# Every load and store on SyncE's queue, and a table in place of the list scheduler

## The chip, the cores and the metric

The kernel runs on one core of a Trainium2 chip. The metric is device time in microseconds of one execution; the median of several runs is compared. PE is TensorE, DVE VectorE, ACT ScalarE, POOL GpSimd, SP SyncE.

## The reference

Three stages follow one another on two batches of 768 positions and 512 channels.

```python
# 1: attention with 8 heads of 64; a score counts only where the 6 hash bits agree
q_bucket = sum((q @ proj > 0) * 2**arange(6));  k_bucket likewise
s = where(q_bucket == k_bucket, q @ k.T / 8, -1e9)
x = softmax(s) @ v
# 2: four causal attentions (experts) of 64 channels, weighted by a top-2 gate
for e in range(4):
    a = softmax(causal((x @ wq[e]) @ (x @ wk[e]).T / 8))
    out += gate_e * (a @ (x @ wv[e]) @ wo[e])
# 3: mix with the position before, square of relu, and a sigmoid gate
xk = mu_k * x + (1 - mu_k) * x_prev;   xr = mu_r * x + (1 - mu_r) * x_prev
return sigmoid(xr @ w_r) * (maximum(xk @ w_k, 0)**2 @ w_v)
```

The weights w_k, w_r and w_v of the third stage come in double precision, all else in single.

## The kernel before

The work is cut into twelve units of 128 positions (six for each batch). For each unit there are four lists of steps: the query (`query_steps`: load, hash, turn), the hashed attention (`lsh_steps`, eight heads), the experts (`moe_steps`, four heads) and the mixing (`mix_steps`: hidden layer h, gate r, down projection v). Matmul operands are split into a high and a low half of 16 bits, and each product is three matmuls. Keys and values of a batch are prepared by `key_steps`, the weights by `split_w` (single precision) and `split_d` (double precision; loads of 512 KB into the tile `raw`, of which there are two).

A head goes through `softmax`: PE writes its scores to PSUM (tile s, or se for an expert), DVE evicts them with the row's extreme (P), ACT takes the exponential (P again, with the row's sum), ACT (in two heads of eight POOL) makes the high half and POOL the low half (PHL), and a DMA transpose on SP's queue makes PT, the stationary operand of the product with v (tile x, or y for an expert). There are four buffers of P, six of PHL, three of PT. Names like PT_5_0 mean unit 5, head 0; PT_m3_1 is unit 3, expert 1; the last number in an order's row is a running number.

Nothing is issued while the steps are run: `Program.add` records each instruction as an `Op` with what it depends on (matmuls of one step in a row form one Op; 2673 in all). Before, `Program.plan` then runs a list scheduler: it has a cost for each Op (`cost`), a due time for each step (`times`, with numbers in `CONF`) and a model of the queues, and leaves a sequence in `self.order`. `issue` emits the Ops in that sequence, each to its engine's queue, where they run in order; all instructions therefore carry the line of `issue` (L396) in the profile, and are told apart by their tiles.

Three switches in CONF name the queue of the DMAs: all 2, which is ACT's.

```python
QS = [nc.sync, nc.gpsimd, nc.scalar]
def DQ():      # weights
    return QS[CONF["dq"]]
def LQ(i):     # keys, values and queries: SP for what comes first
    return QS[CONF["lq"]] if i else nc.sync
def OQ():      # outputs
    return QS[CONF["oq"]]
```

Of the kernel before, what the change touches and what calls it, by code (L numbers as in the profile page):

```python
# [131 lines left out]
class Op:  # L132

    __slots__ = ("eng", "calls", "prio", "uses", "after", "before", "step", "ahead", "left", "ready", "end", "dur", "dma", "lock",
                 "table", "tiles")


class Program:
# [3 lines left out]
    def __init__(self, nc):  # L142
        self.nc, self.ops, self.ahead, self.last, self.share = nc, [], (), None, 1.0
        self.step = Step(self, None)
        self.step.at = -3.0
# [4 lines left out]
    def add(self, engine, method, args, kw):  # L150
# [4 lines left out]
        if not (eng == "PE" and o is not None and o.eng == "PE" and o.step is self.step):  # L155
            o = Op()
            o.eng, o.calls, o.uses, o.step, o.ahead = eng, [], {}, self.step, self.ahead
            o.after, o.dur, o.dma, o.lock, o.table = set(), 0.0, 0.0, False, None
            self.ops.append(o)
            self.last = o  # L160
        o.calls.append((engine, method, args, kw))
        self.cost(o, method, args, kw, views)
# [17 lines left out]
    def switch(self, ns):  # L180

        self.last.dur += ns

    def cost(self, o, method, args, kw, views):

        n = max((v.ids.size for v, _ in views), default=1)
        psum = any(v.tile.pool.psum for v, _ in views)
        ins = [v for v, w in views if not w and v.ids.size > 1]
        if o.eng == "PE":
            x = args[2] if method == "matmul" else args[1]  # L190
            cols = x.ids.size if method == "matmul" else 128
            o.dur += max(cols / 2.4 * (2 if x.dt == F32 else 1) + 2.5, 26.0) * self.share * 1.015
        elif method.startswith("dma_start"):
            v = views[0][0]
            size = v.ids.size * mybir.dt.size(v.dt)
            if method == "dma_start":
                dram = next(a for a in args if not isinstance(a, View))
                run = dram.ap[-1][1] * mybir.dt.size(dram.dtype)
                o.dur, o.dma = 60.0, 250.0 + size * 128 * 2.67e-3 * (1.5 if run <= 256 else 1.0) + (600.0 if run <= 16 else 0.0)
            else:  # L200
                o.dur, o.dma = 1100.0 + size / 256 * 27.0, size / 256 * 150.0
        elif o.eng == "DVE":
            rate = 1.043
            if not psum and len(ins) < 2 and "accum_out" not in kw and method in ("tensor_scalar", "tensor_copy"):
                rate = 0.53 if any(v.dt == F32 for v in ins) else 0.26
                o.lock = n > 1
            elif method == "tensor_copy" and all(v.dt == F16 for v, _ in views):
                rate = 0.53
            elif not psum and len(ins) > 1:
                o.lock = True  # L210
            o.dur = (143.0 if n > 20 else 140.0) + rate * n + (80.0 if "accum_out" in kw else 0.0) - 78.0
        elif o.eng == "ACT":
            o.dur = (150.0 if psum else 190.0) + 0.83 * n + (187.0 if "accum_out" in kw else 0.0) - 94.0
            f = args[2] if method == "activation" else None
            o.table = f if f in (AF.Exp, AF.Sigmoid) else None
        elif o.eng == "POOL":
            o.dur = 147.0 + (1.9 if len(ins) > 1 else 0.85) * n
            o.lock = True

    def plan(self, conf):  # L220

        window, wait = conf["win"], conf["wait"]
        lat = {"DVE": 130.0, "ACT": 145.0, "POOL": 135.0, "PE": 75.0, "SP": 60.0}
        for o in self.ops:
            o.before, o.left, o.ready = [], len(o.after), 0.0
            o.prio = o.step.at - sum(conf[a] for a in o.ahead)
            o.tiles = [t for t in o.uses if t.slot]
            for t in o.tiles:
                t.users = 0
        free, queue, opened = {}, {}, set()  # L230
        for o in reversed(self.ops):
            for q in o.after:
                q.before.append(o)
                q.prio = min(q.prio, o.prio - 1e-6)
        for o in self.ops:
            for t in o.tiles:
                t.users += 1
                if t not in opened:
                    opened.add(t)
                    free.setdefault(t.slot, [0.0] * t.bufs)  # L240
                    queue.setdefault(t.slot, []).append((o.prio, len(opened), t))
        for q in queue.values():
            q.sort(key=lambda a: a[:2], reverse=True)
        ends = {t: 0.0 for t in opened}
        held = set()
        todo = {e: [] for e in lat}
        clock = {e: 0.0 for e in lat}
        lock = 0.0
        slow, frame, busy = False, 0, {}
        table = AF.Exp  # L250
        order = []

        now, lines, coming, lanes = 0.0, ([], []), [], []
        inf = float("inf")

        def done(o, end):
            o.end = end
            for q in o.before:
                q.left -= 1
                q.ready = max(q.ready, end + (-170.0 if q.eng == o.eng == "PE" else lat[q.eng]))  # L260
                if not q.left:
                    l = todo[q.eng]
                    k = len(l)
                    while k and l[k - 1].prio > q.prio:
                        k -= 1
                    l.insert(k, q)
            for t in o.tiles:
                t.users -= 1
                ends[t] = max(ends[t], end)
                if not t.users:  # L270
                    free[t.slot].append(ends[t])

        for o in self.ops:
            if not o.left:
                todo[o.eng].append(o)
        for l in todo.values():
            l.sort(key=lambda o: o.prio)
        while len(order) < len(self.ops):
            best = None
            for e, l in todo.items():  # L280
                pick = None
                for o in l[:window]:
                    at = max(clock[e], o.ready)
                    if pick is not None and at + wait.get(e, 0.0) >= pick[0]:
                        continue
                    if o.dma:
                        if len(lanes) >= 7:
                            if not lanes[-7].end:
                                continue
                            at = max(at, lanes[-7].end)  # L290
                        if e == "SP" and sum(1 for d in lanes[-6:] if not d.end and d.eng == "SP") > 2:
                            continue
                    new = [t for t in o.tiles if t not in held]
                    if len(new) == 1:
                        t = new[0]
                        if not free[t.slot] or queue[t.slot][-1][2] is not t:
                            continue
                        at = max(at, min(free[t.slot]))
                    for t in new if len(new) > 1 else ():
                        same = [u for u in new if u.slot == t.slot]  # L300
                        if len(free[t.slot]) < len(same) or any(a[2] not in same for a in queue[t.slot][-len(same):]):
                            at = None
                            break
                        at = max(at, sorted(free[t.slot])[len(same) - 1])
                    if at is None:
                        continue
                    if pick is None or at + wait.get(e, 0.0) < pick[0]:
                        pick = (at, o)
                if pick and (best is None or pick[0] < best[0]):
                    best = pick  # L310

            limit, landed = best[0] if best else inf, None
            while landed is None and (lines[0] or lines[1] or coming):
                rate = 0.42 if lines[0] and lines[1] else 1.0
                step, kind = limit - now, None
                for k in (0, 1):
                    if lines[k] and lines[k][0][0] / rate <= step:
                        step, kind = lines[k][0][0] / rate, k
                if coming and max(coming[0][0] - now, 0.0) <= step:
                    step, kind = max(coming[0][0] - now, 0.0), 2  # L320
                if kind is None:
                    for k in (0, 1):
                        if lines[k]:
                            lines[k][0][0] -= max(step, 0.0) * rate
# [854 lines left out]
```

## Time and profile before

| | |
|---|---|
| median of 3 runs | 524.77 us (524.51 to 527.95) |
| span of the profiled execution | 523.5 us; its own time was not noted apart, the median is 1.3 us more |
| PE busy | 443.3 us, 85% |
| DVE busy | 378.4 us, 72% |
| ACT busy | 349.1 us, 67% |
| POOL busy | 311.6 us, 60% |

A busy share is a mean over the whole span. The kernel has a start in which keys, values and weights are brought in and split, a long middle in which all twelve units overlap, and a short end; which engine sets the time differs between them, so the shares have to be read by stages. The idle time of an engine that nobody waits for costs nothing.

### The profile page before, as it was taken

The page shows a single profiled execution, that of the slowest core. Times are in us where ns is not written, and L with a number is a line of the kernel's source. Part 1 is how long each engine was busy: PE and PEld are TensorE (multiplying, and loading weights), DVE is VectorE, ACT ScalarE, POOL GpSimd, SP SyncE. Part 2 cuts the span into 40 slices and gives each one's busy share as a digit, 9 for nine tenths or more (in the row PEclk, how much of TensorE's full clock was granted, in tenths as well). Part 3 has the DMA queues.
Part 4 walks back from the last instruction along what each step waited for, and adds up shares of the span by engine and source line. Part 5 has one row for each costly group of instructions (what it writes and reads, how often), then busy time and mean ns, then how long its engine had stood idle before and what let it go on. Part 6 is the DMA issues. An engine that isn't in the chain of part 4 may idle for free.

```text
span 523.5 us, 15721 instructions
## 1 busy us (share of the span) xinstructions
PE 443.3 (85%) x6288; PEld 335.6 (64%) x6288; DVE 378.4 (72%) x1094; ACT 349.1 (67%) x660; POOL 311.6 (60%) x286
## 2 busy tenths in 40 slices
PE   1666655486679899898898999998999999998997
PEld 1644454374466685685777678786786867876764
DVE  2789878688889958766987976866857687376432
ACT  3358855677777857956378977886665978558231
POOL 5879762755756934946464693962936568374110
PEclk9977879878899999999899999999999999999999
DMA  8749979599879996998479889496554889847200
GB/s 245 185 123 172 241 168 221 131 196 193 134 140 207 152 172 87 150 191 147 107 162 155 163 140 163 96 183 99 118 111 90 132 149 174 126 84 117 68 23 20
DMA packets 225243, 75.08 MB, mean 143 GB/s; under 512 B 216593, under 2 KB 220817, under 8 KB 225169
## 3 DMA queue, kind: packets, MB, share of 16 engines
q1 hardware_dynamic: 198288, 52.19, 60.0%
q10 hardware_dynamic: 26880, 21.88, 15.9%
q8 instruction: 49, 0.80, 0.6%
q14 instruction: 26, 0.20, 0.1%
HBM read 22.14 MB, written 3.15 MB: 48 GB/s over the span
## 4 chain that ended last, share of the span: by engine, by line
PE 40%; DMA 15%; DVE 13%; issue 9%; ACT 9%; POOL 7%; SPq 1%; ACTq 0%; POOLq 0%; DVEq 0%
DMA PT<-PHL 9%; PE h L396 8%; PE v L396 7%; PE s L396 5%; DMA PT_m<-PHL_m 5%; PE x L396 4%; PE r L396 4%; POOL PHL L396 3%; PE qk L396 3%; POOL PHL_m L396 2%; DVE P L396 2%; ACT P L396 2%; PE tr_x L396 2%; PE o L396 1%; DVE P_m L396 1%
## 5 line engine op out<-in xcount | busy, mean ns | idle before, releaser
L396 POOL TENSOR_TENSOR PHL<-P,PHL 128x768 f16<-128x768 f32 x96 | 159.1, 1667 | 56.2 <-ACT PHL L396 48.9
L396 DVE TENSOR_SCALAR_CACHE_REDUCE P<-s 128x768 f32<-128x768 f32 x96 | 91.1, 952 | 22.7 <-PE s L396 16.7
L396 ACT ACTIVATE P<-P,mx 128x768 f32<-128x768 f32 x96 | 89.1, 929 | 27.4 <-DVE mx L396 26.4
L396 PE MATMUL s<-y,x 128*128 128x384 f16 x384 | 81.7, 342 | 18.0 <-DVE P L396 13.4
L396 PE MATMUL x<-v,PT 128*128 128x64 f16 x1728 | 68.9, 197 | 11.4 <-DMA PT<-PHL 9.2
L396 PEld LDWEIGHTS <-PT 128*128 128x128 f16 x1728 | 63.6, 101 | 21.9 <-DMA PT<-PHL 12.7
L396 PE MATMUL h<-mk,WK 128*128 128x128 f16 x1152 | 74.7, 219 | 2.5 <-POOL mk L396 1.9
L396 PE MATMUL v<-WV,k 128*128 128x512 f16 x288 | 71.7, 379 | 0.7 <-DVE kT L396 0.7
L396 PEld LDWEIGHTS <-WK 128*128 128x128 f16 x1152 | 67.7, 98 | 7.0 <-issue 2.3
L396 PEld LDWEIGHTS <-x 128*128 128x128 f16 x576 | 42.0, 100 | 46.0 <-issue 24.9
L396 POOL TENSOR_TENSOR PHL_m<-P_m,PHL_m 128x128 f16<-128x128 f32 (+5 forms) x48 | 48.9, 1037 | 29.2 <-ACT PHL_m L396 28.6
L396 ACT ACTIVATE PHL<-P 128x768 f16<-128x768 f32 x72 | 59.8, 835 | 6.8 <-DMA PT_m<-PHL_m 4.1
L396 PE MATMUL qk<-xT,WQK 128*128 128x128 f16 x576 | 42.8, 229 | 3.6 <-DVE xT L396 1.9
L396 PEld LDWEIGHTS <-WQK 128*128 128x128 f16 x576 | 37.5, 103 | 6.8 <-issue 4.6
L396 PEld LDWEIGHTS <-k 128*128 128x128 f16 x288 | 26.1, 98 | 23.1 <-DVE kT L396 0.8
L396 ACT ACTIVATE P_m<-P_m,bias_m 128x128 f32<-128x128 f32 (+5 forms) x48 | 31.7, 660 | 11.2 <-DVE P_m L396 11.2
L396 PE MATMUL r<-WR,mr 128*128 128x512 f16 x144 | 36.6, 379 | 0.7 <-DVE e L396 0.7
L396 DVE TENSOR_SCALAR_CACHE_REDUCE P_m<-se 128x128 f32<-128x128 f32 (+5 forms) x48 | 28.6, 617 | 6.7 <-PE se L396 5.0
L396 ACT ACT_TABLE_LOAD x20 | 25.7, 1283 | 10.1 <-DMA consts<-in_consts_dram 7.1
L396 POOL TENSOR_TENSOR mr<-m32r,mr 128x512 f16<-128x512 f32 x12 | 13.9, 1159 | 30.4 <-ACT mr L396 30.4
L396 PE MATMUL y<-vn,PT_m 128*128 128x64 f16 x504 | 22.6, 195 | 8.5 <-DMA PT_m<-PHL_m 8.5
L396 PEld LDWEIGHTS <-PT_m 128*128 128x128 f16 x504 | 19.9, 99 | 14.7 <-DMA PT_m<-PHL_m 10.4
(127 smaller groups left out, 808.3 us busy)
## 6 DMA issues: line engine op xcount, KB each, us to landing
raw_k<-in_moe_w_k_dram ACTq DMA_DIRECT2D x8, 512.0 KB, 4.9
raw_v<-in_moe_w_v_dram ACTq DMA_DIRECT2D x8, 512.0 KB, 5.2
out_dram<-e ACTq DMA_DIRECT2D x12, 256.0 KB, 2.3
q<-in_q_dram ACTq DMA_DIRECT2D x11, 256.0 KB, 5.2
raw_r<-in_moe_w_r_dram ACTq DMA_DIRECT2D x4, 512.0 KB, 3.9
k<-in_k_dram SPq DMA_DIRECT2D x4, 384.0 KB, 6.0
v<-in_v_dram SPq DMA_DIRECT2D x4, 384.0 KB, 4.0
PT<-PHL SPq DMA_TRANSPOSE x96, 4.7
```

The costliest lines, as they stand in the source:

```text
L396: getattr(getattr(self.nc, engine), method)(*[real(a) for a in args], **{k: real(a) for k, a in kw.items()})
```

## The change

Two things change. All loads of weights, keys, values and queries, and the twelve stores of the output, are issued on SP's queue, on which the transposes are too: 66 DMAs leave ACT's queue, which keeps six small ones (the hash's projection, constants, mu). And the list scheduler goes, with its costs, due times and CONF; a table of 2673 numbers gives the sequence of the Ops. The Ops, their tiles and what they depend on are the same in both, and so are the numbers of instructions of each engine, except that ACT's table loads are 18 and no longer 20.

```diff
+    def arrange(self, table):
+        places = np.frombuffer(zlib.decompress(base64.b85decode("".join(table.split()))), np.uint16)
+        self.order = [self.ops[i] for i in places]
...
-    def LQ(i):
-        return QS[CONF["lq"]] if i else nc.sync
...
+    LOADS = nc.sync
...
         for dap, sap in src_dmas:
-            DQ().dma_start(dap(w32), sap)
+            LOADS.dma_start(dap(w32), sap)
...
-        DQ().dma_start(raw.rearrange("p n a -> p (n a)"), src.bitcast(U32))
+        LOADS.dma_start(raw.rearrange("p n a -> p (n a)"), src.bitcast(U32))
...
-                OQ().dma_start(out[b, s0:s0 + P, :], o)
+                LOADS.dma_start(out[b, s0:s0 + P, :], o)
...
-    nc.plan(CONF)
+    nc.arrange(ORDER)
...
+ORDER = """
+c-jrsgMwf=5CFhN(n-IyZQJ(D+O}=mwr$(CZQHi(y{n%nfiOT&0MY_L2FL>p=^#B6hrD3GLVhR=86gwo1BA@rAPW?Mq7VY1;30s5PzXwaLTQ)?lb{4lh
...
```

On SP's queue, this stood in a row where unit 1's heads are transposed, before:

```order
L396 DMA_TRANSPOSE PT_1_0_878<-PHL_1_0_788 128x12x128
L396 DMA_TRANSPOSE PT_1_1_908<-PHL_1_1_828 128x12x128
L396 DMA_TRANSPOSE PT_1_2_939<-PHL_1_2_842 128x12x128
L396 DMA_TRANSPOSE PT_1_3_1055<-PHL_1_3_882 128x12x128
L396 DMA_TRANSPOSE PT_1_4_1097<-PHL_1_4_886 128x12x128
L396 DMA_TRANSPOSE PT_1_5_1149<-PHL_1_5_942 128x12x128
L396 DMA_TRANSPOSE PT_1_6_1217<-PHL_1_6_973 128x12x128
L396 DMA_TRANSPOSE PT_1_7_1300<-PHL_1_7_997 128x12x128
L396 DMA_TRANSPOSE PT_m0_0_1360<-PHL_m0_0_1236 128x2x128
L396 DMA_TRANSPOSE PT_m0_1_1395<-PHL_m0_1_1243 128x2x128
```

and now, from the sixth of that unit's heads on:

```order
L188 DMA_TRANSPOSE PT_1_5_1095<-PHL_1_5_960 128x12x128
L188 DMA_TRANSPOSE PT_1_7_1180<-PHL_1_7_954 128x12x128
L188 DMA raw_r0_0_1199<-in_moe2_w_r_dram 128x1024
L188 DMA_TRANSPOSE PT_1_0_1242<-PHL_1_0_893 128x12x128
L188 DMA_TRANSPOSE PT_1_4_1297<-PHL_1_4_1097 128x12x128
L188 DMA raw_r1_0_1300<-in_moe2_w_r_dram 128x1024
L188 DMA_TRANSPOSE PT_1_3_1336<-PHL_1_3_1059 128x12x128
L188 DMA_TRANSPOSE PT_1_2_1376<-PHL_1_2_1111 128x12x128
L188 DMA raw_r2_0_1409<-in_moe2_w_r_dram 128x1024
L188 DMA_TRANSPOSE PT_m0_1_1449<-PHL_m0_1_1280 128x2x128
L188 DMA_TRANSPOSE PT_m0_0_1459<-PHL_m0_0_1360 128x2x128
L188 DMA raw_r3_0_1479<-in_moe2_w_r_dram 128x1024
```

Loads of the gate's weights (raw_r, 512 KB each) now stand between the transposes, and the heads of a unit come in another sequence. Over the whole queue 29 loads stand ahead of the first transpose (nine before; five of the 29 are of raw_k), and behind it fifteen weight loads of 512 KB, loads of queries, keys and values and the twelve stores stand between transposes.

On PE's queue, this stood before between the scores of unit 5's head 0 (s_5_0) and the first matmul that reads a PT of that unit (one row of each step; weight loads and repeated rows are left out):

```order
L396 MATMUL s_5_0_3341<-y1_0_0_418,x1_5_3048 128x384
...
L396 MATMUL vg_3_3348<-WVG_234,xT_3_2913 128x260
...
L396 MATMUL s_5_1_3364<-y1_0_0_418,x1_5_3048 128x384
...
L396 MATMUL v_1_3260<-WV2_1925,k2_1_2929 128x512
...
L396 MATMUL se_3_1_3390<-kT_0_1125,qT_3_3142 128x512
...
L396 MATMUL s_5_2_3404<-y1_0_0_418,x1_5_3048 128x384
...
L396 MATMUL h_2_0_3437<-mk_2_3308,WK2_655 128x128
...
L396 MATMUL s_5_3_3455<-y1_0_0_418,x1_5_3048 128x384
...
L396 MATMUL s_5_4_3477<-y1_0_1_254,x1_5_3048 128x384
...
L396 MATMUL y_3_3484<-vn_0_1181,PT_m3_0_3410 128x64
...
L396 MATMUL s_5_5_3544<-y1_0_1_254,x1_5_3048 128x384
...
L396 MATMUL x_5_3594<-v_0_0_399,PT_5_0_3464 128x64
```

and now, for the head that this unit uses first, head 7:

```order
L188 MATMUL s_5_7_3340<-y1_0_1_300,x1_5_2746 128x384
...
L188 MATMUL x_4_3015<-v_0_0_269,PT_4_3_3315 128x64
...
L188 MATMUL h_1_4_3405<-mk_1_2566,WK2_208 128x128
...
L188 MATMUL s_5_2_3439<-y1_0_0_400,x1_5_2746 128x384
...
L188 MATMUL s_5_5_3521<-y1_0_1_300,x1_5_2746 128x384
...
L188 MATMUL vg_4_3544<-WVG_442,xT_4_3512 128x260
...
L188 MATMUL s_5_6_3569<-y1_0_1_300,x1_5_2746 128x384
...
L188 MATMUL v_1_3332<-WV2_1806,k2_1_3131 128x512
...
L188 MATMUL qk_4_3599<-xT_4_3512,WQK_272 128x128
...
L188 MATMUL s_5_3_3689<-y1_0_0_400,x1_5_2746 128x384
...
L188 MATMUL o_3_3707<-yT_3_3687,WO_195 128x128
...
L188 MATMUL x_5_3782<-v_0_1_387,PT_5_7_3765 128x64
```

More steps of other units, mixing (h, v), projections (qk, vg, o) and products of unit 4's heads (x_4), lie between a head's scores and its product.

On DVE's queue, the first evictions of unit 0 stood before so:

```order
L396 TENSOR_SCALAR P_0_0_491,mx_0_492<-s_0_0_479 128x768
L396 TENSOR_SCALAR P_0_1_500,mx_0_492<-s_0_1_485 128x768
L396 TENSOR_SCALAR mx_0_492<-mx_0_492 128x1
L396 SCALAR_TENSOR_TENSOR naq_1_503<-q32_1_396,naq_1_503 128x8x64
L396 TENSOR_SCALAR mx_0_492<-mx_0_492 128x1
L396 TENSOR_SCALAR P_0_2_519,mx_0_492<-s_0_2_495 128x768
L396 SCALAR_TENSOR_TENSOR v_0_1_305<-v32_0_1_1_416,v_0_1_305 128x768
L396 TENSOR_SCALAR mx_0_492<-mx_0_492 128x1
L396 TENSOR_SCALAR P_0_3_547,mx_0_492<-s_0_3_510 128x768
```

and now so:

```order
L188 TENSOR_SCALAR P_0_2_437,mx_0_438<-s_0_2_423 128x768
L188 TENSOR_SCALAR P_0_0_444,mx_0_438<-s_0_0_432 128x768
L188 TENSOR_SCALAR mx_0_438<-mx_0_438 128x1
L188 TENSOR_SCALAR wd_k20_0_461<-wm_k20_0_398 128x512
L188 TENSOR_SCALAR mx_0_438<-mx_0_438 128x1
L188 COPY x1_0_366<-tr_x1_0_312 128x512
L188 COPY x2_1_466<-tr_x2_1_446 128x512
L188 TENSOR_SCALAR P_0_3_473,mx_0_438<-s_0_3_468 128x768
L188 COPY x2_1_466<-tr_x2_1_446 128x512
L188 COPY y1_0_0_400<-tr_y1_0_0_0_1_478 128x768
L188 SCALAR_TENSOR_TENSOR wd_k20_0_461<-raw_k20_0_372,wd_k20_0_461 128x512
```

Work on the weights of the hidden layer (wd_k) has moved in among the first evictions, and the splitting of values and of the next query out of them.

## Rows read from the trace of the kernel before

**Rows 1.** The page's first part: busy time, share and instructions of each engine.
```profile
PE 443.3 (85%) x6288; PEld 335.6 (64%) x6288; DVE 378.4 (72%) x1094; ACT 349.1 (67%) x660; POOL 311.6 (60%) x286
```

**Rows 2.** Busy time by stages; columns: stage, its length, engines, granted clock, DMA, GB/s.
```profile
0.00:32.00 32.00, 14.20 (x226) 12.86 (x227) 17.56 (x40) 11.55 (x16) 22.27 (x31) 0.94 0.77 200
32.00:157.00 125.00, 82.99 (x1094) 62.19 (x1092) 104.92 (x280) 87.68 (x174) 81.97 (x77) 0.85 0.86 174
157.00:497.00 340.00, 323.34 (x4756) 245.73 (x4753) 247.69 (x759) 243.24 (x460) 205.05 (x177) 0.99 0.79 136
497.00:524.00 27.00, 22.80 (x221) 14.80 (x219) 8.22 (x17) 6.62 (x11) 2.32 (x2) 0.98 0.06 21
```

**Rows 3.** Waits of PE, 0 to 160 us: total, times, longest.
```profile
PE s L396 <- DVE P L396: 12.8, 13, 2.0
...
PE y L396 <- DMA PT_m<-PHL_m: 4.6, 2, 2.4
PE x L396 <- DMA PT<-PHL: 4.3, 3, 2.1
```

**Rows 4.** Waits of PE, 157 to 524 us, the longest three.
```profile
PE x L396 <- DMA PT<-PHL: 4.9, 6, 1.2
PE y L396 <- DMA PT_m<-PHL_m: 4.0, 5, 1.5
PE tr_y L396 <- DVE nbk L396: 1.4, 1, 1.4
```

**Rows 5.** The chain, 30 to 160 us: its shares and two pieces (start, length).
```profile
by line: issue 18.3%; POOL PHL L396 11.0%; DMA PT_m<-PHL_m 8.2%; DMA raw_v<-in_moe_w_v_dram 5.5%; DVE P L396 4.7%; ACT P L396 4.7%; DVE wd_k L396 4.3%; DMA PT<-PHL 4.1%; DVE wd_r L396 2.8%; ACT PHL L396 2.5%; PE s L396 2.0%; DVE x L396 1.9%
...
88.62 4.51 issue
...
142.76 7.09 DMA raw_v<-in_moe_w_v_dram
```

**Rows 6.** The page's groups: busy, mean ns, idle before with what ended it.
```profile
L396 POOL TENSOR_TENSOR PHL<-P,PHL 128x768 f16<-128x768 f32 x96 | 159.1, 1667 | 56.2 <-ACT PHL L396 48.9
L396 DVE TENSOR_SCALAR_CACHE_REDUCE P<-s 128x768 f32<-128x768 f32 x96 | 91.1, 952 | 22.7 <-PE s L396 16.7
L396 ACT ACTIVATE P<-P,mx 128x768 f32<-128x768 f32 x96 | 89.1, 929 | 27.4 <-DVE mx L396 26.4
L396 PE MATMUL s<-y,x 128*128 128x384 f16 x384 | 81.7, 342 | 18.0 <-DVE P L396 13.4
L396 PE MATMUL x<-v,PT 128*128 128x64 f16 x1728 | 68.9, 197 | 11.4 <-DMA PT<-PHL 9.2
...
L396 PE MATMUL h<-mk,WK 128*128 128x128 f16 x1152 | 74.7, 219 | 2.5 <-POOL mk L396 1.9
L396 PE MATMUL v<-WV,k 128*128 128x512 f16 x288 | 71.7, 379 | 0.7 <-DVE kT L396 0.7
...
L396 ACT ACTIVATE PHL<-P 128x768 f16<-128x768 f32 x72 | 59.8, 835 | 6.8 <-DMA PT_m<-PHL_m 4.1
```

**Rows 7.** The tile PT: its transposes on SP (min/median/max ns), and issue to landing.
```profile
L396 SPq DMA_TRANSPOSE PT<-PHL x96: 1413/1600/6159, 40.0 to 451.9; - x96
...
DMA to landing us min/median/max: 3.6/4.7/9.4
```

**Rows 8.** The tile raw_v: its loads on ACT's queue, same columns.
```profile
L396 ACTq DMA_DIRECT2D raw_v<-in_moe_w_v_dram x8: 334/335/363, 113.2 to 163.1; - x8
```

**Rows 9.** The page's groups: loads of ACT's function table.
```profile
L396 ACT ACT_TABLE_LOAD x20 | 25.7, 1283 | 10.1 <-DMA consts<-in_consts_dram 7.1
```

**Rows 10.** Waits of SP's queue, 30 to 160 us, the longest.
```profile
SPq L396 <- PE x L396: 40.6, 14, 9.7
```

More of the change, by code (lines that the diff above doesn't have):

```diff
@@ L1 @@
+import base64
+import zlib
 from contextlib import ExitStack
@@ L132 @@
 class Op:
-    __slots__ = ("eng", "calls", "prio", "uses", "after", "before", "step", "ahead", "left", "ready", "end", "dur", "dma", "lock",
-                 "table", "tiles")
+    __slots__ = ("eng", "calls", "uses", "after", "step")
 class Program:
@@ L142, in __init__ @@
     def __init__(self, nc):
-        self.nc, self.ops, self.ahead, self.last, self.share = nc, [], (), None, 1.0
+        self.nc, self.ops, self.last = nc, [], None
         self.step = Step(self, None)
-        self.step.at = -3.0
     def __getattr__(self, name):
@@ L156, in add @@
             o = Op()
-            o.eng, o.calls, o.uses, o.step, o.ahead = eng, [], {}, self.step, self.ahead
-            o.after, o.dur, o.dma, o.lock, o.table = set(), 0.0, 0.0, False, None
+            o.eng, o.calls, o.uses, o.step = eng, [], {}, self.step
+            o.after = set()
             self.ops.append(o)
@@ L178, in add @@
                 log.append((o, m))
[L180 to L324, printed above, removed]
-                    now = max(now, limit)
-                    break
-                for k in (0, 1):
-                    if lines[k]:
-                        lines[k][0][0] -= step * rate
-                now += step
-                if kind == 2:
-                    o = coming.pop(0)[1]
-                    lines[o.calls[0][1] == "dma_start"].append([o.dma, o])
-                else:
-                    landed = lines[kind].pop(0)[1]
-            if landed is not None:
-                done(landed, now + conf["dm"])
-                continue
-            if best is None:
-                raise RuntimeError("the plan is stuck at %d of %d" % (len(order), len(self.ops)))
-            at, o = best
-            e = o.eng
-            todo[e].remove(o)
-            for t in o.tiles:
-                if t not in held:
-                    held.add(t)
-                    queue[t.slot].pop()
-                    free[t.slot].remove(min(free[t.slot]))
-            order.append(o)
-            if o.dma:
-                clock[e] = at + o.dur
-                o.end = 0.0
-                lanes.append(o)
-                coming.append((at + 1960.0, o))
-                coming.sort(key=lambda a: a[0])
-                continue
-            if o.lock:
-                start = max(at + 120.0, lock) - 120.0
-                end = start + o.dur
-                lock = end
-            else:
-                end = at + o.dur
-            if e == "PE":
-                while frame < at // 3413:
-                    share = busy.get(frame, 0.0) / 3413
-                    slow = share < 0.88 if slow else share < 0.43
-                    frame += 1
-                end = at + o.dur * (2.2 if slow else 1)
-                a = at
-                while a < end:
-                    b = min(end, (a // 3413 + 1) * 3413)
-                    busy[a // 3413] = busy.get(a // 3413, 0.0) + b - a
-                    a = b
-            if e == "ACT" and o.table is not None and o.table != table:
-                table = o.table
-                end += 1400.0
-            clock[e] = end
-            done(o, end + 170.0 if e == "PE" else end)
-        while lines[0] or lines[1] or coming:
-            if not (lines[0] or lines[1]):
-                now = max(now, coming[0][0])
-                o = coming.pop(0)[1]
-                lines[1].append([o.dma, o])
-            k = 0 if lines[0] else 1
-            w, o = lines[k].pop(0)
-            now += w
-            done(o, now)
-        self.order = order
-        return max(o.end for o in order)
@@ L408, in __call__ @@
             p = self.program
-            old = p.step, p.ahead
-            p.step, p.ahead = self, ()
+            old = p.step
+            p.step = self
             self.f()
-            p.step, p.ahead = old
+            p.step = old
 class Engine:
@@ L456, in dps @@
         return ps_d.tile(shape or [P, 512], F32, tag="d", name=name)
-    def ahead(what, f, *a):
-        old, nc.ahead = nc.ahead, nc.ahead + (what,)
-        r = f(*a)
-        nc.ahead = old
-        return r
     def hi_part(eng, dst, src, sc=1.0):
@@ L825, in lsh_steps @@
             if h < H:
-                steps.append(lambda h=h: ahead("hs", score, h))
+                steps.append(lambda h=h: score(h))
             if h >= LAG:
-                steps.append(lambda h=h: ahead("hp", pv, h - LAG))
-        steps.append(lambda: ahead("hf", fin))
+                steps.append(lambda h=h: pv(h - LAG))
+        steps.append(lambda: fin())
         LS[i] = [once(f) for f in steps]
```

206 lines of the change are left out of this document (93 added, 113 removed).

## The prediction

> **What bounds the kernel now.** I read the page's busy shares first, then the busy time by stages, and then, within a stage, the waits of the engines and the chain. TensorE (PE) is busy for 443.3 us of the span of 523.5 [rows 1], so 80.2 us of it are idle. The table by stages shows where [rows 2]: from 0 to 32 us PE is busy for 14.2 us, from 32 to 157 for 83.0 of 125.0 (42.0 idle), from 157 to 497 for 323.3 of 340.0 (16.7 idle), and in the last 27 for 22.8. The stages are bound by different things. In the second one VectorE (DVE) has 104.9 us of work in 125.0, 20.1 idle, and PE's clock is granted at only 0.85: here PE waits for others. In the third PE is nearly full at 0.99, and only its 16.7 us of idle time can be won by any order of the same instructions.
>
> What PE waits for differs too. In the first 160 us the softmax's evictions on DVE lead (12.8 us), and the transposed tiles, PT and PT_m, cost 4.3 and 4.6 us [rows 3]. After 157 us those two are the only waits above 1.5 us, with 4.9 and 4.0 us [rows 4]. The chain from 30 to 160 us is a patchwork: 18.3% of it is "issue", with one piece of 4.51 us at 88.62, and it holds one wait of 7.09 us for a load of raw_v at 142.76 [rows 5]. ScalarE (ACT) issued that load, so when it was issued was a matter of its place in ACT's queue.
>
> **The chain that an order has to cover.** A head's scores become a stationary tile of PE through five steps, at these durations [rows 6]: DVE's eviction 0.95 us, ACT's exponential 0.93, ACT's upper half 0.84, GpSimd's lower half 1.67, then the DMA transpose, which lands 4.7 us after its issue (median) [rows 7]. That is 9.1 us if nothing queues. PE needs that much other work between a head's scores and its product with v.
>
> **The change, part by part.** The matmuls, evictions, activations and bytes are the same; 66 DMAs change queue, and every engine gets another sequence.
>
> *Loads and stores leave ACT.* Issuing one takes ACT's queue 0.334 us [rows 8], so 66 of them give back 22.1 us of it. ACT has 243.2 us of work in the 340 of the third stage and 87.7 in the 125 of the second, so it is not the bound of either; I count nothing for this by itself. It is worth something only where ACT stands on the chain, in the early stage, and goes into that term. Two table loads go as well, 2 x 1.28 us [rows 9], beside idle time of ACT: 0. If that cover were gone it would be 2.6 us.
>
> *Early stage, 32 to 157 us.* The most that a better order can win there without taking work from DVE is DVE's idle time, 20.1 us. Of the chain's pieces, the two named above (7.09 + 4.51 = 11.6 us) are queueing and not work, and both are of the kind that a new order and a free ACT queue alter. I take half of the bound, **-10 us**, close to those 11.6. The ends: 0, for the DVE work ahead of the first finished unit is nearly the same (with each instruction at its duration in the trace, 147.4 us stand on DVE ahead of the last matmul of unit 0's down projection before, 149.4 after); and -20.
>
> *Third stage, 157 to 497 us.* I counted, in both orders, PE's work between a head's last score matmul and the first matmul that reads its PT, each matmul priced at its group's busy time over its count (s 0.213 us, x 0.040, h 0.065, v 0.249 [rows 6], the rest likewise from their groups), and scaled so that the whole gives the 443.3 us. For the first head that unit 5 uses, this lead grows from 13.4 to 20.0 us (the order in the section on the change shows what stands between). By sixths of the 144 heads the median is 10.6, 18.3, 17.8, 16.1, 15.6, 13.5 us before and 10.7, 20.4, 25.1, 24.0, 19.5, 22.7 after: longer everywhere but in the first sixth. That should take away waits on PT and PT_m, 8.9 us in this stage. Against it stands the ring of three PT buffers: a transpose can't be issued before the head three places ahead has been multiplied. The work between that release and the use is 7.3 us before and 6.6 after in the median, and the cases in which it is less than a transpose's 4.7 us rise from 27 to 31, among the later two thirds from 7 to 14. So the lead is longer in a part of the chain that the ring cuts off. I take a bit less than half of the 8.9, **-4 us**; the ends are -16.7 (all idle time) and +8 (twice as many short gaps, twice the waits).
>
> *Loads between the transposes.* The new wait is this: a weight load of 512 KB (raw_k, raw_r, raw_v) waits for its buffer, of which there are two, to be released by DVE and ACT, and it now waits on SyncE's (SP's) queue. Behind it stand the next transposes, and PE waits for those. Fifteen such loads stand after the first transpose, where before there was none on that queue; five more and all other early loads stand ahead of it. The trace of before has no load between transposes. From below, 0: SP itself sat waiting for PE to release PT for 40.6 us in 30 to 160 [rows 10], so a load issued in such a pause delays nothing. From above, 512 KB at the 200 GB/s of the first stage [rows 2] take 2.6 us, fifteen of them 39 us, of which at most about half can show on PE, whose lead there (10.7 us) is little over the chain's 9.1: 20 us. The nearest row is that of the waits on PT early, 4.3 us; I take two thirds of that, **+3 us**. The 12 stores and the loads of q, k and v also stand in this queue; these wait for buffers that have long been free, or for the last step of a unit, and I count them at 0, covered by the same pauses.
>
> At the end nothing moves that I can price: after the last transposes PE has 22.8 us of work in 27 [rows 2], and the last output still waits for its whole down projection.
>
> One rule of the skill bears on the queues. The Trainium skill, "DMA: Bandwidth & Descriptors", in "Rules for kernel authors", says that spreading DMAs over the issuing engines gains no bandwidth, since all run on the same 16 DMA engines, and saves only issue time. By that rule alone, moving 66 issues onto one queue costs SP 66 x 0.334 = 22 us of issue time (an estimate) and no bandwidth; if that reached the end undiminished the sum below would be 22 us higher. The pauses of SP in the row above speak against that, and the sum goes without it.
>
> **The sum.** 523.5 - 10 - 4 + 3 = 512.5 us of span. The times shown have a median of 524.8, 1.3 us above the span of the profiled execution, so 513.8, rounded: **514 us**, 2.1% less.
>
> **Rivals.** *Loads hold the transposes (slower).* Place: SP's queue from 30 to 180 us, where the fifteen weight loads stand. A load whose buffer isn't released yet stops every transpose behind it, PT arrives late, PE idles, DVE gets its scores later, and releases the next raw buffer later still. Price: the upper end above, +20, with no early gain, and -4 later: 539.5 + 1.3 = 541 us. It decides once PE's waits on PT and PT_m in the first 160 us, 8.9 now, pass some 20 us. For it: the lead in the first sixth has not grown, and the chain already has a load of 7.09 us in it. Against it: SP's long pauses, and that most loads of raw_k come before the transposes.
>
> The Trainium skill, same page, "Queues, rings and completion order", says that SP and ACT each own a ring of their own on the same DMA engines, and that an engine alternates between the rings with work by packets. By it, a transpose behind a load on one ring also waits for that load's bytes, which works toward this rival's price; no run so far shows such a pair.
>
> *DVE's floor (no change).* The early stage stays at 125 us because DVE has the same work ahead of the first finished unit, and only the third stage wins: 523.5 - 4 + 2 + 1.3 = 523 us. For it: DVE's 84% there and the 147.4 against 149.4 us. Against it: 20.1 us of idle time on that very engine.
>
> *Nearly all idle time goes (much faster).* Early -20, third stage -13, loads 0: 490.5 + 1.3 = 492 us. For it: the leads of 20 to 25 us, twice the chain. Against it: the ring of three.
>
> That the change doesn't do what it says can be excluded for the queues, since the order shows each load on SP.
>
> **How the numbers follow.** Forecast 0.55, DVE's floor 0.17, loads hold the transposes 0.15, much faster 0.13. About 1% (5 us) is what a measurement of this kernel can tell from no change. The forecast and the much faster case are faster: 0.68; the floor at 523 is the same: 0.17; the loads are slower: 0.15. The range of 494 to 532 us takes in the forecast with its ends of either term (502 to 524), the floor, the milder half of the loads' case and the nearer half of the much faster one, and leaves out about 0.15.
>
> **What would show it.** Early term: PE's idle time in the first 160 us falls from 60 to about 50, and unit 0's last down projection comes some 10 us earlier. Third stage: PE's waits on PT and PT_m there fall below 6 us. Loads: SP's waits for a release of raw (by DVE or ACT) appear and are a few us on PE's side; the median landing of a transpose stays within half a us of 4.7. I am wrong if those landings or waits grow to tens of us, or if PE's work becomes longer by a lower clock: a new order can leave pauses that bring the granted clock down, as in the early stage now, and I have no term for that.

## The result

The change makes the kernel slower, by a little: 530.73 us against 526.82 (medians of 14 runs each), a ratio of 1.0085 (95% interval 1.0059 to 1.011). Forecast were 514 us. The profiled execution has a span of 528.8 us, 5.3 more than before.

The page's first part and the busy time by stages of the kernel after, in the columns of [rows 1] and [rows 2]:

```profile
PE 447.6 (85%) x6288; PEld 337.5 (64%) x6288; DVE 375.3 (71%) x1094; ACT 351.8 (67%) x658; POOL 313.1 (59%) x286
```

```profile
0.00:32.00 32.00, 18.08 (x232) 14.98 (x233) 24.65 (x53) 15.45 (x23) 20.42 (x29) 1.00 0.82 227
32.00:157.00 125.00, 86.62 (x1192) 64.84 (x1190) 102.33 (x303) 88.40 (x178) 86.64 (x84) 0.86 0.89 179
157.00:497.00 340.00, 314.90 (x4637) 240.72 (x4635) 238.74 (x721) 241.41 (x448) 203.81 (x172) 0.98 0.75 131
497.00:529.00 32.00, 28.05 (x237) 16.95 (x235) 9.62 (x19) 6.56 (x11) 2.27 (x2) 1.00 0.07 26
```

The two early stages got better: PE is busy for 7.5 us more of the first 157 than in [rows 2]. The third got worse: PE is idle for 25.1 us of it (16.7 before), and the granted clock is 0.98 in place of 0.99. Busy time counts a slow matmul as more work, so I also counted PE's matmuls at fixed prices by their width, those of stretches at full clock (0.16 us for 384 columns, 0.029 for 64; 397.6 us in all), and asked how much is done at a given time; with other such prices the differences move by up to 2 us. The second column is before, the others stand against it (the last four are experiments, below):

```
 us  before  after   e2     e3     e4     e5
 40   13.3   +1.2   +0.3   +1.2   +0.6   +1.2
160   73.3   +5.6   +1.0   +6.6   +4.0   +4.0
180   91.1   +1.8   +1.1   +3.3   -3.3   +3.6
220  126.6   -1.4   +0.7   +3.1   -5.1   +1.8
320  211.7   +0.3   +4.8   +6.4   -3.6   +5.2
380  266.1   -4.0   +6.3   +6.5   -7.1   +0.3
440  323.3   -8.0   +6.3   +6.3  -11.0   -3.4
500  378.2   -5.4   +6.5   +6.9   -9.8   -0.6
```

After the change PE is 5.6 us ahead at 160 us, has lost that by 220, and loses 8 more between 320 and 440. So the questions are what takes the lead away, and whether the queue or the order does it.

PE's waits after the change, before 160 us (total, times, longest), the longest, for [rows 3]:

```profile
PE x L188 <- DMA PT<-PHL: 19.9, 10, 3.9
```

and from 157 to 500 us, the first five, for [rows 4]:

```profile
PE tr_x L188 <- DVE x L188: 7.4, 4, 4.0
PE x L188 <- DMA PT<-PHL: 4.7, 6, 1.2
PE qk L188 <- DVE k L188: 2.7, 2, 2.1
PE qk L188 <- DVE kT L188: 1.8, 1, 1.8
PE y L188 <- DVE y L188: 1.5, 1, 1.5
```

Early, PE waits for PT far more than before (4.3 us). Late, the wait for PT has stayed (4.9 before) and that for PT_m has nearly gone (0.6 us, 4.0 before), but a wait of tr_x for DVE's x has come, with one of 4.0 us. Transposes still land as they did, for [rows 7]:

```profile
DMA to landing us min/median/max: 3.6/4.4/7.4
```

### The profile page after: what moved, and what is told of

Same layout as the page of the kernel before. It is cut to its first block, busy times and chain, and to the rows that moved or that the text cites. A ratio compares the mean times of both kernels' runs of the same rounds, so it can differ in the third digit from the quotient of the medians.

```text
span 528.8 us, 15675 instructions
## 1 busy us (share of the span) xinstructions
PE 447.6 (85%) x6288; PEld 337.5 (64%) x6288; DVE 375.3 (71%) x1094; ACT 351.8 (67%) x658; POOL 313.1 (59%) x286
## 5 line engine op out<-in xcount | busy, mean ns | idle before, releaser
L188 PE MATMUL x<-v,PT 128*128 128x64 f16 x1728 | 67.0, 197 | 24.8 <-DMA PT<-PHL 24.6
L188 PE MATMUL s<-y,x 128*128 128x384 f16 x384 | 85.9, 356 | 1.9 <-DVE P L188 1.0
L188 PEld LDWEIGHTS <-PT 128*128 128x128 f16 x1728 | 61.2, 100 | 33.8 <-DMA PT<-PHL 28.8
L188 POOL TENSOR_TENSOR PHL_m<-P_m,PHL_m 128x128 f16<-128x128 f32 (+5 forms) x48 | 50.4, 1052 | 41.0 <-ACT PHL_m L188 38.5
L188 PE MATMUL v<-WV,k 128*128 128x512 f16 x288 | 68.5, 382 | 0.0
L188 PE MATMUL qk<-xT,WQK 128*128 128x128 f16 x576 | 38.9, 225 | 10.7 <-DVE kT L188 5.7
L188 PEld LDWEIGHTS <-WQK 128*128 128x128 f16 x576 | 35.5, 101 | 13.7 <-issue 9.9
L188 PE MATMUL r<-WR,mr 128*128 128x512 f16 x144 | 34.4, 379 | 1.1 <-DVE g L188 1.1
L188 POOL TENSOR_SCALAR PHL<-P 128x768 f16<-128x768 f32 x24 | 20.0, 833 | 17.2 <-ACT P L188 16.7
L188 PEld LDWEIGHTS <-PT_m 128*128 128x128 f16 x504 | 19.8, 98 | 14.2 <-issue 8.0
L188 DVE SCALAR_TENSOR_TENSOR h<-h,t 128x512 f32<-128x512 f32 x24 | 16.7, 695 | 16.7 <-ACT t L188 16.6
```

The lines of the kernel that those rows point to most:

```text
L188: getattr(getattr(self.nc, engine), method)(*[real(a) for a in args], **{k: real(a) for k, a in kw.items()})
```

## The experiments

All but e1, e7 and e12 have all 66 loads and stores on SP. Where an order is changed, only the table of places differs, and a mixture of two orders holds every dependence. In all, before ran at 525.8 to 527.0 us.

**e1 and e2: the queue without the order, the order without the queue.**

```diff
-    LOADS = nc.sync
+    LOADS = nc.scalar        # e1; the first k, v, q stay on nc.sync
-ORDER = (the table)
+ORDER = (the list scheduler's sequence, as a table)   # e2
```

> The table's order kept, the 66 loads and stores back on ACT's queue. In the trace of the change, PE is 5.6 us of its own work ahead of before at 160 us and 8 us behind at 440. Theory J (joints): the order lost it in the third stage, where it left little PE work between a unit's last product and the transpose of its normalized rows (tr_x waits for DVE's x, 7.4 us in four waits) and at the projections behind it (qk waits for kT and k, 4.5 us); then the queue is beside the point and this is within 2 us of the change, 529 to 533 us. Theory Q (queue): loads and stores on SP's queue hold the transposes (PE's waits on PT before 160 us are 19.9 us, 4.3 before); then this gives back 5 us or more, 525 or less.

> The list scheduler's order kept, the 66 loads and stores on SP's queue. J: the order is what counts, so this is within 2 us of before, 523 to 528 us. Q: 5 us or more slower than before, 531 us or more.

e1 took 571.1 us (1.0821, 1.0771 to 1.0871), e2 516.8 (0.9822, 0.9786 to 0.9857). Both theories miss in both runs. With the list scheduler's order, moving the queue is a gain of 9.1 us (the later expectations say 9.4, the ratio on 526.8), the very opposite of Q; so with the loads on SP the order costs 14 us, more than J had it, and with them on ACT 45 (571.1 against 525.9 for before). The table can't do without SP: with its loads on ACT it is 40 us slower. In the profile of e1 ACT itself waits for weights (two of its four longest waits, of an execution with a span of 575.9 us):

```profile
ACT wm_k L188 <- DMA raw_k<-in_moe_w_k_dram: 19.9, 7, 4.2
...
ACT wm_v L188 <- DMA raw_v<-in_moe_w_v_dram: 11.7, 4, 3.5
```

A load in ACT's queue is issued only when ACT has come that far, and ACT then waits for what is left of its landing (4.7 us in the median for raw_k in e1). The third stage of e2, for the third line of [rows 2], and PE's waits in it:

```profile
157.00:497.00 340.00, 326.86 (x4803) 249.05 (x4801) 248.92 (x762) 244.67 (x463) 205.06 (x177) 1.00 0.76 134
```

```profile
PE x L188 <- DMA PT<-PHL: 2.0, 4, 0.7
PE y L188 <- DMA PT_m<-PHL_m: 1.8, 2, 1.2
```

PE's waits on PT and PT_m there are 3.8 us where they were 8.9 [rows 4]: with the 66 DMAs out of ACT's queue, the same order brings the heads sooner. The table of work done says the same: +1.0 us at 160, +6.3 at 380. By which way they cost that much in ACT's queue is not shown. Their issues take 26.9 us in the trace of before (0.334 us is the price of a 512 KB load, the others have medians of 0.36 to 0.45), but 14.2 us of that lie beside a running instruction of ACT. An issue that waits for its buffer with ACT's next work behind it, or a load that comes late, may cost more than the issues.

**e3 and e4: halves of the two orders.**

```diff
-ORDER = (the table)
+ORDER = (the table's groups started by 160 us, then the others in the list scheduler's sequence)   # e3
+ORDER = (the list scheduler's groups started by 170 us, then the others in the table's sequence)   # e4
```

> The table's order for what it had started by 160 us (844 groups), then the list scheduler's order for the rest; all loads and stores on SP. J: the 5.6 us of lead at 160 us are kept, and the third stage is that of before: 518 to 522 us, faster than both. Q: stores and late loads still hold the transposes, so at most half of the lead is kept: 524 us or more.

> The reverse: the list scheduler's order for what it had started by 170 us (853 groups), then the table's; all loads and stores on SP. J: the early stage is that of before, the third loses what the change lost there, 8 to 13 us: 533 to 539 us, slower than both. Q: between before and the change, 525 to 531 us.

e3: 517.5 us (0.9807, 0.976 to 0.9855); e4: 535.5 (1.0183, 1.0147 to 1.0219). J's ranges hold (e3 lies just below its own), Q's don't. Against e2 the table's head brings nothing (its lead of 6.6 us at 160 is 3.3 at 180, and at 380 both are level), and its tail costs 19. So what the order loses, it loses after 160 us. Part of e4's 19 us is the seam: it falls from +4.0 to -3.3 between 160 and 180 us.

**e5 and e6: the halves of a turn.** The wait of tr_x for DVE's x is not the joint that J named. The tile is tr_x1_7, a query's rows being turned, in two halves of four transposes, each copied out by DVE. This is PE after the change around it (start, duration, what; in brackets the idle time before it):

```profile
257.42 0.81 PE L188 MATMUL s<-y,x 128*128 128x384 f16 x4
258.07 0.39 PE L188 MATMUL tr_x<-consts,nbq 128*128 128x128 f16 x4
262.43 0.38 PE L188 MATMUL tr_x<-consts,nbq 128*128 128x128 f16 x4 [3.97 <-DVE x L188]
262.65 0.60 PE L188 MATMUL y<-vn,PT_m 128*128 128x64 f16 x15
263.09 1.44 PE L188 MATMUL s<-y,x 128*128 128x384 f16 x4
```

and DVE, which had other things to do before the copy:

```profile
257.40 2.39 DVE L188 SCALAR_TENSOR_TENSOR v<-v,v 128x768 f16<-128x768 f32 x1
...
260.90 0.95 DVE L188 TENSOR_SCALAR_CACHE_REDUCE P<-s 128x768 f32<-128x768 f32 x1
261.77 0.08 DVE L188 DVE_READ_ACCUMULATOR P<-s 128x1 f32 x1
261.89 0.15 DVE L188 TENSOR_SCALAR mx<-mx 128x1 f32<-128x1 f32 x1
261.96 0.41 DVE L188 COPY x<-tr_x 128x512 f16<-128x512 f16 x1
```

The two halves lie in one PSUM tile. The list scheduler's order has them in a row; the table puts DVE's copy of the first between them in 18 of 24 turns, and the second half then waits for that copy, though it writes elsewhere in the tile. The copy ends at 262.37, PE goes on at 262.43. And the wait costs more than its 4.0 us (busy time by stretches, same columns as above; the last three figures of a line are granted clock, DMA and GB/s):

```profile
258.00:262.00 4.00, 0.46 (x6) 0.28 (x5) 3.93 (x9) 2.44 (x6) 3.29 (x2) 1.00 1.15 163
262.00:266.00 4.00, 3.57 (x28) 1.90 (x28) 2.29 (x7) 3.68 (x8) 2.54 (x3) 0.64 0.86 178
266.00:270.00 4.00, 4.00 (x34) 2.28 (x33) 3.48 (x7) 2.43 (x4) 3.17 (x2) 0.93 0.43 118
```

After PE has stood still, the clock is granted at 0.64 in the mean of the next four us, between the levels of 1.2 and 2.4 GHz, and a head's four score matmuls take 1.44 us where they took 0.81 before the wait. The Trainium skill, "PSUM — Partial Sum Buffer", section "PSUM bank collisions raise a hardware error", says that the compiler's scheduler adds a dependency between any two instructions on different engines that touch the same bank and quadrant. The trace agrees: the second half waits for a copy of other columns; which software put that wait into this program it doesn't show.

```diff
 PE   tr_x1_7 (first half)
+PE   tr_x1_7 (second half)                      # e5: in the 18 turns; e6 does the reverse in all 24
 DVE  x1_7 <- tr_x1_7 (first half)
-PE   tr_x1_7 (second half)
```

> The table's order with one thing undone: in 18 of the 24 turns of a query the table has DVE's copy of the first half between the two halves of the transpose on PE (tr_x1, tr_x2); here the second half follows the first at once, as in the list scheduler's order. Theory H (halves): both halves lie in one PSUM tile, so the second waits for the copy, and PE's waits of tr_x on DVE's x (11.4 us, 4.0 and 7.4 before and after 160 us; 3.1 in before, of another kind) are the price: 519 to 524 us. Rival B (buffers): the loss is spread over the waits behind buffers that this order holds longer (PHL lives 73 groups in the mean, 34 before; qk waits for a PSUM buffer): 527 us or more.

> The reverse, on the list scheduler's order with all loads on SP (516.8 us): in all 24 turns the second half of the transpose is put behind DVE's copy of the first. H: 18 such turns cost 7 to 11 us there, so 24 cost 9 to 15: 526 to 532 us. B: the copies are early enough, 520 us or less.

e5: 524.75 us (0.9981, 0.9952 to 1.001), 6.0 less than the change. e6: 524.2 (0.9976, 0.9952 to 1.0), 7.4 more than e2. Both times lie between the two ranges, nearer to H's: H holds in sign in both directions, and the price is a little less than it had (7 to 11 and 9 to 15 us). e5 also gives a turn's PSUM buffer back earlier (one second half moves by 95 places); in e6 none moves by more than twelve, and it costs as much. In e5 the wait of tr_x for x is down to 0.2 us. In e6 it is 10.0 us before 160 us, where e2 has 4.2:

```profile
PE tr_x L188 <- DVE x L188: 10.0, 6, 4.7
```

A good part of the price shows in the clock. Its mean over an execution, in the median of the runs, rises from 0.956 to 0.963 with e5 and falls from 0.955 (e2) to 0.947 with e6; 0.7% of PE's 445 us are some 3 us (an estimate). In e6's profiled execution PE is not idle for longer than in e2's (72.9 and 75.2 us) but busy for longer (449.4 and 441.7).

**e8: the same halves in the head alone.**

> The order that was the table's until 160 us and the list scheduler's after (517.5 us), with the halves together in the nine turns of the head where the table parts them. H: the 4.0 us of such waits before 160 us go, 513 to 515 us, the fastest. B: 516 to 518 us.

517.5 us (0.9857, 0.9819 to 0.9895), as e3 and as B had it: no gain. Before 160 us, where PE waits for others anyway, these waits cost nothing in that order.

**e7, e12 and e13: what the queue gives.**

```diff
 e7:   weights on nc.sync; q, k, v of later units and the stores on nc.scalar
 e12:  weights on nc.scalar; all others on nc.sync
 e13:  (kernel before)  -dq=2, lq=2, oq=2   +dq=0, lq=0, oq=0
```

> The list scheduler's order with only the loads of weights on SP's queue (31 DMAs); queries, the second batch's keys and values and the stores stay on ACT's. All 66 on SP gave 9 us. Theory W (weights): what helps is that a weight load no longer waits for its place in ACT's queue: 516 to 519 us. Rival L (later ones): PE is only 1.0 us ahead of before at 160 us, when nearly all weights are in, and 6.3 at 380, so the loads and stores of the third stage are what costs on ACT: 522 to 526 us.

> The list scheduler's order; weights load on ACT's queue as before, the loads of queries, keys and values and the stores go on SP's. All on SP gave 9.4 us, the weights alone 5.6 us. If the two parts add up, this gives the other 4: 521 to 523 us. If each alone already gives most of it, 518 to 520.

> The kernel before with its three switches set to SP, so that the list scheduler plans anew with all loads and stores there. If the gain of 9.4 us comes from ACT's freed queue and not from a lucky order, a new plan keeps it: 513 to 519 us. If the numbers in CONF only fit the old plan, 520 us or more.

(The 31 DMAs of e7's expectation are those that stay on ACT's queue; 35 loads of weights go on SP's.) e7: 520.7 us (0.9899, 0.9853 to 0.9944); e12: 526.3 (0.996, 0.9918 to 1.0001, not to be told from no change); e13: 536.3 (1.0197, 1.0156 to 1.0238). The weights give more than half, between W and L. By their ratios the two parts alone, some 5.3 and 2.1 us, come to less than the 9.4 of both, but the intervals allow that they simply add. And the gain belongs to the list scheduler's old sequence: planned anew for SP, with the numbers in CONF that were found for the other queue, the kernel is 10 us slower than before. Its second stage shows it, with 78.0 us of PE in 125 where [rows 2] has 83.0, and 0.77 of the clock.

**e9 and e10: where the other 8 us are.** e5 still stands 8.0 us above e2. By the table of work done it is level with e2 at 320 us (+5.2 and +4.8) and 9.7 behind at 440.

```diff
+ORDER = (e5's groups started by 325 us, then the others in the list scheduler's sequence)   # e9
+ORDER = (the list scheduler's groups started by 300 us, then the others in e5's sequence)   # e10
```

> The table's order with the halves together (524.8 us) for what had started by 325 us (1719 groups), then the list scheduler's for the rest; all loads and stores on SP. In the traces the former is level with the list scheduler's order on SP (516.8 us) at 320 us and 9.7 us of PE's work behind at 440. Theory M (middle): the rest of the loss arises after 320 us, where this order has PE wait in many small pieces for PT and for PSUM buffers: 514 to 518 us. Rival D (debt): it is laid up before, in heads and mixing steps left over, and is paid later whatever order follows: 521 us or more.

> The reverse: the list scheduler's order for what it had started by 300 us (1549 groups), then the table's with the halves together. M: 524 to 528 us. D: 516 to 519 us.

e9: 519.1 us (0.9875, 0.983 to 0.992), 5.7 of the 8 us back, between M and D and nearer to M. e10: 539.9 (1.0291, 1.0233 to 1.0348), far above both: against e2 its trace loses some 16 us of PE's work at the seam, between 280 and 320, and some 9 more from there to 440, as e5 does. So most of the loss arises in that stretch, after either head; some 2 us of e9 stay open. In it PE has 11.2 us of idle time in e5 and 1.5 in e2 (300 to 445 us, first e5, then e2):

```profile
300.00:445.00 145.00, 133.78 (x2072) 103.59 (x2070) 100.10 (x331) 105.68 (x211) 89.14 (x77) 1.00 0.80 136
```

```profile
300.00:445.00 145.00, 143.47 (x2148) 110.47 (x2146) 102.17 (x332) 112.41 (x217) 95.15 (x82) 1.00 0.77 134
```

No engine is full in e5. Its waits of PE there, the first five, are many and small. A third is for PT; in the others DVE writes a tile that the waiting step doesn't read (qk has no use for kT), which I read as a wait for a PSUM buffer that DVE reads there:

```profile
PE x L188 <- DMA PT<-PHL: 3.9, 5, 1.3
PE qk L188 <- DVE kT L188: 1.8, 1, 1.8
PE y L188 <- DVE y L188: 1.7, 1, 1.7
PE y L188 <- DVE mx L188: 1.0, 1, 1.0
PE y L188 <- DVE rse L188: 0.7, 1, 0.7
```

**e14, e15, e16: are they slips of place?**

```diff
-PE   qk_8 (waits 1.8 us), v_4, v_4, ...
+PE   v_4, v_4, ..., qk_8            # the waiting step behind the next 1 to 3 us of independent work
```

> The table's order with the halves together (524.8 us) and ten steps of PE that waited 0.5 to 1.8 us between 300 and 446 us (qk, y, x) moved behind the next 1.2 to 2.8 us of PE's work that does not depend on them. In that stretch PE is idle for 11.2 us there and for 1.5 us in the list scheduler's order on SP. Theory L (local): each is a slip of place, a step that stands just ahead of its PSUM buffer's release or of its PT; moved, most of the ten waits (9.8 us together) go, 517 to 521 us. Rival G (chain): buffers and the chain behind them are behind PE there as a whole, and the waits come back at the next step: 523 us or more.

> The same for 19 waits from 157 to 446 us. L: some 3 to 6 us below the run with the ten alone, 513 to 518 us. G: 522 us or more.

> The same on the list scheduler's order with all loads on SP (516.8 us), whose third stage has 13 waits of 0.4 to 1.4 us, 10 us together. L: 510 to 514 us, below all others. G: 515 to 518 us.

e14: 526.5 us (0.9994, 0.9966 to 1.0023); e15: 530.1 (1.0076, 1.0042 to 1.011); e16: 519.3 (0.9859, 0.9818 to 0.99). L falls: none is faster than what it started from (524.8, 524.8, 516.8). e15 is clearly slower; e14 and e16 can't be told from their starts. In the trace of e15 PE is still idle for 10.7 us from 300 to 445 us, with 2.8 us in one wait of qk: the waits came back, as G has it.

**e17, e18, e19: is it missing filler?** From 300 to 445 us both orders turn almost as many heads (54 transposes in e5, 53 in e2), but the table has PE do 46 us of mixing (h, v, r) beside them and the list scheduler's order 58.

```diff
+ORDER = (e5's, the mixing on all engines taken forward to where the list scheduler has it)   # e17
+ORDER = (the list scheduler's, the mixing held back to where the table has it)               # e18
+PE   v_4 x6 x2, qk_8     # e19: ready mixing matmuls put ahead of a waiting step, PE's queue alone
```

> The table's order with the halves together (524.8 us), and from about 290 us on the steps of the mixing (h, r, v with their steps on the other engines, in their own sequence) taken forward, so that each comes when the attention and the experts are as far as they are in the list scheduler's order. In the traces 80 us of mixing are done on PE there when the rest has got 180 us far, in the table's order when it has got 212. Theory F (filler): both orders turn 53 or 54 heads from 300 to 445 us, which is the pace of the chain, but the table gives PE 46 us of mixing to do beside them and the list scheduler's order 58; PE idles for the difference and does the rest at the end, where it is full anyway. Then this gains most of the 8 us: 516 to 520 us. Rival G: the heads' sequence itself is what is slow there: 523 us or more.

> The reverse: the list scheduler's order with all loads on SP (516.8 us), and from about 260 us on the mixing held back to where it comes in the table's order. F: it loses 6 to 12 us, 523 to 529 us. G: 515 to 519 us.

> The table's order with the halves together (524.8 us). At nine of the ten waits between 300 and 446 us, 1.3 to 2.6 us of mixing matmuls (h, r, v) whose inputs and PSUM tile were there by the trace, but which stood behind the waiting step in PE's queue, are put ahead of it; only PE's queue changes, 22 steps. Theory F (filler): the time of those waits (9.2 us) is used, and PE has that much less to do at the end: 516 to 521 us. Rival G: the heads' chain is what sets the pace, and filled waits only move: 523 us or more.

e17 took 638.6 us and e18 661.4. Both are wrecks and decide nothing; why they are so slow was not looked into. e19: 525.0 us (0.9984, 0.9945 to 1.0023), as e5. F falls too in this form: the nine waits that were filled are mostly gone, others have come (x_8 2.4 us, x_11 2.0), and PE is idle for 9.8 us of the stretch in place of 11.2:

```profile
300.00:445.00 145.00, 135.17 (x2055) 104.21 (x2054) 99.00 (x328) 105.63 (x211) 90.16 (x77) 0.99 0.82 135
```

So a wait that is filled or moved comes back at another step. I read it so that in this stretch the chain of heads sets the pace in the table's order, and PE's own work in the list scheduler's; which link of the chain does it stays open. One thing in the traces fits, and no run has tested it: from 157 to 500 us the heads stand ready, from the end of PHL to the issue of their transpose, for 658 us in sum and 3.9 in the median in e5, and for 251 and 1.45 in e2. It is not that SP's queue waits longer for one of the three PT buffers. For PE's x and y, which release one, it waits 66.2 us there in e5 and 61.8 in e2 (first e5, then e2):

```profile
SPq L188 <- PE x L188: 36.2, 26, 5.5
...
SPq L188 <- PE y L188: 30.0, 16, 3.7
```

```profile
SPq L188 <- PE x L188: 51.3, 38, 4.4
...
SPq L188 <- PE y L188: 10.5, 12, 1.8
```

What differs is the sequence. With each row paired to its step, e2 issues the transposes in the very order in which their heads became ready; in e5 105 pairs stand the other way round, so that a finished head waits in SP's queue behind one that is not: 97 of the 658 us pass while the first transpose in the queue still waits for its own PHL, none of the 251. e14, e15 and e19 left SP's queue as it was. An order of the transposes by readiness, the rival that this leaves, wasn't tried, and neither was a fourth PT buffer.

## Why the prediction was wrong

The step that failed is **the third stage, -4 us**. It priced only PE's waits on PT and PT_m. These did fall, from 8.9 to 5.3 us (4.7 and 0.6), but the term had nothing for other waits, nor for the clock, and their sum turned its sign: PE's idle time in the stage grew by 8.4 us, and by the table of work done PE went from 5.6 us ahead at 160 to 5.4 behind at 500, 11 us lost where 4 were to be won. I had seen the ring of three cut the longer lead off, with an end of +8, and took the other sign. Against the list scheduler's order on the same queue, the runs put +14 us in its place: 6.0 of it (e5) from a wait that I didn't price at all, a PE step behind a DVE copy of the same PSUM tile, with the drop of the clock after it; the other 8 mostly after 320 us, where the heads' chain seems to set the pace and the cause is open. The longer lead is there, but as time in which finished heads wait for their transpose.

**Early, -10 us:** PE had done 5.6 us more by 160 us, about half; its idle time of the first 157 fell from 59.8 to 52.3 us. But the gain is no gain at the end: with the list scheduler's order behind it the same head ends where e2 ends (e3, e8). Being early in a stage isn't the same as finishing earlier: from 157 to 445 us PE is then idle for 14.8 us in e3 and for 11.2 in e2.

**Loads between the transposes, +3 us, and loads off ACT, 0:** together +3, where the queue measured -9.1 us with the list scheduler's order (e2). I took ACT for free since it is not full; but it makes P and PHL, and without the DMAs in its queue the heads came sooner. The feared wait did come with the table (PE on PT 19.9 us before 160, the rival's own mark of some 20). It did not come with the list scheduler's order on the same queue (4.7 us), which has eighteen loads of 512 KB behind the first transpose, and 11.8 us of it stay when the table's loads are on ACT (e1). So the loads don't make most of it, and it stands in the same slack early stage.

**The rivals:** loads that hold the transposes are refuted by e2 and e1. DVE's floor had the time nearest (523), by another way: the early stage did move. That the measured time lay inside the range (494 to 532) rests on its width, which came from a rival that didn't happen. By the 1% that I took for what a measurement can tell from no change the result would be none; with 14 runs of each, the interval of 1.0059 to 1.011 tells it from none.

Small slips in the sum changed little. The 66 issues took 26.9 us in the trace of before and not 22.1, the ends of the two main terms reach from 501 to 526 us and not from 502 to 524, and the floor's price has +2 for the loads where the forecast has +3.

I had printed the clue without reading it: DVE's rows in the section on the change show the copies of the two halves of x2_1 with an eviction between them.

## What to carry to other kernels

An engine that is not full can still be in the chain: price the DMAs in its queue by whose result is late, not by its busy share. When a new order parts two writes to one PSUM tile, look at what reads the tile between them; that read becomes a wait, and a stall of a few us costs the clock too. Queue and order don't simply add: the table with loads on ACT lost 40 us and a new plan for SP 10, yet the list scheduler's old sequence, made for ACT's queue, was among the fastest with its DMAs on SP (516.8 us, 1.8% below before). So change and measure the two apart. And waits that a term priced can go as forecast while the stage gets slower: look for what the engine waits for instead.

## What the runs showed of the hardware

A matmul that writes other columns of a PSUM tile than those being copied still waited for the copy, by a semaphore of the program: 3.97 us in one case. The granted clock was 1.00 in the four us of that stall and 0.64 in the mean of the four after it. And moving 66 DMAs from ACT's queue, which was 67% busy, to SP's was worth 9.1 us of 526 with the order of everything kept.
